# A DFT and MLP sum on Trainium2: the last block's second column pair is turned in two halves, and the last stores change queues

## The chip, the cores and the metric

The kernel runs on one core of a Trainium2 chip. The metric is device time in microseconds. The core has TensorE (matrix products), VectorE (DVE), ScalarE (ACT), GpSimd (POOL) and SyncE (SP). Transfers are started by SP, ACT and GpSimd and are carried by 16 DMA engines.

## The reference

The input is 2048 rows of 640 numbers. After a layer norm the same rows go through two branches, and both are added to the input:

```python
a = einsum("bsd,ed->bse", xn, dft_hid_re);  b = einsum("bsd,ed->bse", xn, dft_hid_im)
y = einsum("ts,bse->bte", dft_seq_re, a) - einsum("ts,bse->bte", dft_seq_im, b)
h = gelu(einsum("bsd,df->bsf", xn, w1) + b1)
return x + y + einsum("bsf,fd->bsd", h, w2) + b2
```

The first branch is the real part of a discrete Fourier transform over rows and columns; the second is an MLP with 1536 hidden units. Everything is float32.

## The kernel before, in words

The 2048 rows are treated as four blocks of 512 rows. Each float32 product is built from three TensorE passes: operands are split in a high and a low part (`split`, lines 160 and 161), and `product` (lines 277 to 279) adds high by high, high by low and low by high. The MLP comes first and leaves its sums, with x added, in DRAM. Then stages over the sequence direction (`sequence_entry`) alternate with stages over the hidden direction (`hidden_entry`), in an order written out by hand: each stage is a list of entries `n`, TensorE's work for the entry is issued first, and then `hidden_beside(b, n)` returns what the other engines do beside it (the dictionary `post`, by entry number). Engines take their instructions in the order in which they were recorded. There is no planner; a semaphore is waited for where one engine needs another's result.

The last stage handles two blocks at once: `ta`, the other block, and `tb`, the last block. Results stand transposed in PSUM banks, 32 x 32 squares at a time, and have to be turned: `turned` (line 1274 for one bank, line 1277 for two) is a VectorE transpose, `add` (line 428) adds the result to the sum that waits in SBUF, and `store` (line 1254) writes it to the output in four DMAs, one for each quarter of the partitions. A block's 160 columns per quarter are five columns of 32: a first pair, a second pair and a fifth column. A store of a pair moves 128 KB per quarter in runs of 256 bytes; a store of one column moves 64 KB in runs of 128 bytes.

In the last entries of the last stage VectorE does, in this order:

- entries 14 and 15: adds to `v2`, turns it and adds it to the first pair of `tb` (`in_two(0)`, tile `u1`); `out_b(0)` stores it from SP;
- entry 17: `v1` (adds a bank pair to the sum `v1`), `end` (adds a turned piece of the other block to a PSUM bank that TensorE still accumulates onto, and waits for), then turns `v1` as one piece of 1024 columns and adds it to the second pair (`in_two(1)`, tile `u2`); `out_b(1)` stores it, four DMAs from ACT;
- entry 18: `yb4` turns and adds the fifth column of `tb` (tile `y4`) and stores it, four DMAs from GpSimd.

Behind the stages (line 1692) the third column of `ta` is turned and added and stored, two DMAs each from SP and ACT. The fourth waits for TensorE's very last product: one transpose (line 1695), then two DMAs each from SP and ACT. At the very end every engine drains (line 1725), SP waits for all DMAs to land, and GpSimd collects the five engines in a barrier. The second load of the tile that is added to, `load_yb(1)`, comes much earlier, in entry 13.

Of the kernel before, what the change touches and what calls it, by code (L numbers as in the profile page):

```python
# [16 lines left out]
Q = 4  # L17
B = 32
# [8 lines left out]
def kernel(  # L27
# [38 lines left out]
    nc = tc.nc  # L66
    x = x.flatten_outer_dims()
    out = out.flatten_outer_dims()
    S, D = x.shape
    F = w1.shape[1]  # L70
    TB = 512
    NT = S // TB
    NB = TB // B
# [4 lines left out]
    DQ = D // Q  # L78
# [27 lines left out]
    def bank(k):  # L106
        return banks[:, k]
# [35 lines left out]
    def place(tag, shape, dtype=F32R, name=None):  # L143

        return wpool.tile(list(shape), dtype, tag=tag, bufs=1, name=name or tag)
# [24 lines left out]
    def rows_of(ap, t):  # L170
        return ap[t * TB : (t + 1) * TB].rearrange("(n r) d -> r n d", r=B)
# [117 lines left out]
    def hidden(g):  # L289
        i = unit(g)  # L290
        acc = bank(g % 3)
        kinds = ((0, 0), (0, 1), (1, 0))
        steps = [(j, k) for j in range(ND) for k in range(3)]
        if g == 0:
            steps = FIRST
        if g == 1:

            steps.sort(key=lambda s: s[1] == 2)
        for n, (j, k) in enumerate(steps):
            a, b = kinds[k]  # L300
            nc.tensor.matmul(  # L301
                acc, W1[i][:, a, j * P : (j + 1) * P], XT[j][:, b], start=n == 0, stop=n == len(steps) - 1
            )
        return acc
# [47 lines left out]
    A = {}  # L352
# [74 lines left out]
    def add(dst, a, b, op=ALU.add):  # L427
        nc.vector.tensor_tensor(dst, a, b, op=op)
# [23 lines left out]
    def load_a(g):  # L452

        for f in steps_of_load(g):
            f()
# [71 lines left out]
    def f5(u):  # L527
        add(held("ci1", u), held("ci1", u), held("ci2", u))

    def f6(u):  # L530
        add(held("cr1", u), held("cr1", u), held("ci1", u))
# [123 lines left out]
    for tag, size, keys in PLACES:  # L655
        t = whole[tag] = place(tag, (P, size // 4))
# [13 lines left out]
    m = MV[:, 1]  # L670
# [132 lines left out]
    for _ in range(5):  # L803
        y, d, x2, z2, w_ = PB[-1]
# [198 lines left out]
    for g in range(NG):  # L1003
        t, i = divmod(g, NF)
        if t == 0:
# [5 lines left out]
            if i == NF - 1:  # L1011
                open_w()
                acc = hidden(g + 2)
# [11 lines left out]
            else:  # L1025
                acc = hidden(g + 2)
# [7 lines left out]
        elif i < NF - 2:  # L1034
            acc = hidden(g + 2)
# [57 lines left out]
    for q in range(1, NF // 2):  # L1093
        p = q - 1
# [100 lines left out]
    for n in range(1, 2 * NF):  # L1195
        blk, i = divmod(n, NF)
# [39 lines left out]
    def load_part(t, k):  # L1236
        nc.sync.dma_start(new_sum(1, t, k), part_of(t, k))
# [10 lines left out]
            for k in names:  # L1248
                nc.sync.dma_start(part_of(t, k), sums[t, k])

    def store(t, src, c0, c1, on_act=0, queues=None):

        for q in range(Q):
            (queues[q] if queues else nc.scalar if q >= Q - on_act else nc.sync).dma_start(
                rows_of(out, t)[:, :, q * DQ + c0 : q * DQ + c1], src[q * B : (q + 1) * B]
            )

    def reload(lo, w, which="xab"):
# [11 lines left out]
    def turned(acc, name):  # L1270

        if len(acc.shape) == 2:
            yt = A["yt"](name)[:, 0]
            nc.vector.transpose(yt, acc)
        else:
            yt = A["yt"](name)
            nc.vector.transpose(yt.rearrange("p e n -> p (e n)"), acc.rearrange("p e n -> p (e n)"))
        return yt

    def add_turned(dst, yt):  # L1280
        if len(yt.shape) == 2:
            add(dst, dst, yt.rearrange("p (n i) -> p n i", i=B))
        else:
            d = dst.rearrange("p n (e i) -> p e n i", i=B)
            add(d, d, yt.rearrange("p e (n i) -> p e n i", i=B))
# [14 lines left out]
    yo = {}  # L1300
# [183 lines left out]
    def hidden_beside(b, n):  # L1484


        ta, tb = blocks[b - 1][1], blocks[b][1]
        last = b == len(blocks) - 1
        x_, y_, z_ = (banks[:, k : k + 2] for k in (X, Y, Z))
        us, vs = bank(US), bank(VS)  # L1490
        ya = yo[ta]

        def s(which, k):
            return sums[(ta, tb)[which], k]

        def t2(k):
            return lambda: add(s(1, KU[k]), s(1, KV[k]), s(1, KU[k]), ALU.subtract)

        def t3(k):
            return lambda: add(s(0, KU[k]), s(1, KU[k]), s(0, KU[k]), ALU.subtract)  # L1500

        def t4(k):
            return lambda: add(s(0, KV[k]), s(0, KV[k]), s(1, KU[k]), ALU.subtract)

        def columns(k):

            return s(1 if last else 0, ("u1", "u2")[k]).rearrange("p a b -> p (a b)").rearrange("p (n e) -> p n e", n=NB)

        def load_yb(k):
            return lambda: nc.sync.dma_start(columns(k), ys[k][tb])  # L1510

        def copy(dst, src):
            return lambda: nc.scalar.activation(dst, src, AF.Copy)

        def to(dst, acc, name, then=lambda: None):


            def f():
                add_turned(dst, turned(acc, name))
                then()  # L1520

            return f

        def out_a(c0, c1):
            return lambda: store(ta, ya[:, :, c0:c1], c0, c1) if last else None

        def odd():
            yt = turned(us, f"yo_{tb}")
            add_turned(ya[:, :, 4 * B :], yt)
            add_turned(yo[tb, 4], yt)  # L1530
            out_a(4 * B, DQ)()

        def in_two(k):

            acc, name = s(1, ("v2", "v1")[k]), f"yb{k}_{tb}"

            def f():
                if name not in A:
                    A[name] = turned(acc, name)
                else:  # L1540
                    add_turned(columns(k), A.pop(name))
                    out_b(k)()

            return f

        def out_b(k):
            return lambda: store(tb, columns(k), 2 * k * B, 2 * (k + 1) * B, Q if last and k == 1 else 0)

        def last_columns():

            A["end"] = A["rt2"][:, 0, 0, 0]
            nc.vector.transpose(A["end"].rearrange("p (n i) -> p n i", i=B), ya[:, :, 3 * B : 4 * B])

        yb1, yb2 = in_two(0), in_two(1)
        yb4 = to(
            yo[tb, 4], vs, f"yb4_{tb}", lambda: store(tb, yo[tb, 4], 4 * B, DQ, queues=[nc.gpsimd] * Q if last else None)
        )
        f5s = [lambda u=u: f5(u) for u in range(2)] if not last else [lambda: None] * 2
        f6s = [lambda u=u: f6(u) for u in range(2)] if not last else [lambda: None] * 2
        v1 = lambda: add(s(1, "v1"), s(1, "v1"), x_)  # L1560
        end = lambda: add(bank(X + 1), bank(X + 1), A["end"])
        pre = [v1] if n == 17 and not last else []
        post = {

            0: [lambda: gather(1, tb, "v1", z_), lambda: gather(1, tb, "v", vs, op=ALU.subtract), f5s[0]],
            1: [f5s[1]],
            3: [to(ya[:, :, : 2 * B], x_, f"ya1_{ta}")],
            2: [last_columns] if last else [],
            4: [t2(0)],
            5: [t2(1)],  # L1570
            6: [to(ya[:, :, : 2 * B], y_, f"ya2_{ta}", out_a(0, 2 * B)), t2(2)],
            7: [odd],
            8: [t3(0)],
            9: [copy(s(1, "v1"), z_), t3(1)],
            10: [t3(2)],
            11: [t4(0)],
            12: [copy(s(1, "v2"), x_), t4(1)],
            13: [load_yb(0), t4(2), load_yb(1)] if last else [t4(2)],
            14: [lambda: add(s(1, "v2"), s(1, "v2"), z_), yb1],
            15: [yb1] if last else [load_yb(0)],  # L1580
            16: [] if last else [load_yb(1)],
            17: [v1, end, yb2, yb2] if last else [yb1, yb2],
            18: [yb4] if last else [yb2],
            19: [f6s[0]],
            20: [] if last else [f6s[1], yb4],
        }.get(n, [])
        if not last:
            if n in (12, 13):
                post.insert(0, lambda: load_g(b, (NW - 1) * ND + 13 - n))
            if n == 18:  # L1590
                post[:0] = [lambda k=k: load_part(blocks[b + 1][1], k) for k in ("u1", "u")]
            if n == 20:
                post.append(lambda: load_a(put_off[0]))

                def end():
                    to(ya[:, :, 2 * B : 4 * B], x_, f"ya3_{ta}")()
                    store(ta, ya, 0, DQ)

                later.append(end)
        return pre, post  # L1600
# [88 lines left out]


    t = blocks[-2][1]
    for k, queues in ((2, [nc.sync, nc.scalar] * 2), (3, [nc.sync, nc.scalar] * 2)):
        d = yo[t][:, :, k * B : (k + 1) * B]
        if k == 3:
            nc.vector.transpose(d, bank(X + 1).rearrange("p (n i) -> p n i", i=B))  # L1695
        else:
            add_turned(d, turned(bank(X), f"yt_{k}"))
        store(t, d, k * B, (k + 1) * B, queues=queues)
# [31 lines left out]
```

## Time and profile before

| | before |
|---|---|
| median of 3 runs | 854.0 us (853.73 to 854.02) |
| profiled execution, device time | 853.7 us |
| profiled execution, span | 851.9 us |
| TensorE busy | 842.7 us, 99% of the span |
| VectorE busy | 661.1 us, 78% |
| ScalarE busy | 353.6 us, 42% |
| GpSimd busy | 48.1 us, 6% |
| GpSimd's last work before the last stores | ends at 298.4 us |
| granted TensorE clock, mean | 0.998 |

The profiled execution is one run; its device time is 1.8 us longer than the span in which its instructions lie. Times in a timeline are microseconds from the span's start. A timeline row has the start, the duration, the engine, the line, the operation, the tile written and the tile read; `x4` means four such instructions merged in one row, and a duration of a DMA row is the time in which it is issued and described, not in which its bytes move. The time from there until the bytes have landed stands in the rows of DMA issues. SPq and ACTq are the queues of SP and ACT; POOL is GpSimd. A drain is an instruction that ends when its engine's earlier work has ended.

### The profile page before, as it was taken

Reading aid. Unit: us, or ns where it says so; the run is one execution under the profiler, and the core shown is the slowest. Engines: PE = TensorE matmul, PEld = TensorE weight load, DVE = VectorE, ACT = ScalarE, POOL = GpSimd, SP = SyncE. Lnnn points to the kernel's source line nnn. Section 1 sums busy time; section 2 is a strip of 40 time slices with the busy share of each in tenths; the row PEclk is TensorE's granted clock in tenths of the full one; section 3 lists DMA queues with packets and bytes.
Section 4 is the critical chain, followed back from the end, with each engine's and each line's share of the span. In section 5 each row is a group of like instructions: output and inputs, shape, how many; then the busy total and the mean of one; then the engine's idle time right before and its main releaser. Section 6 shows DMA issues by size and latency. Waiting matters only on the chain.

```text
span 851.9 us, 10326 instructions
## 1 busy us (share of the span) xinstructions
PE 842.7 (99%) x3711; PEld 695.8 (82%) x3711; DVE 661.1 (78%) x836; ACT 353.6 (42%) x496; POOL 48.1 (6%) x69
## 2 busy tenths in 40 slices
PE   8999999999999999999999999999999999999997
PEld 6888888878888888888888888888888888888885
DVE  7554766785758888879979787889967998885686
ACT  7443634456666554343444343232323423222241
POOL 0000211031211300000000000000000000000001
PEclk9999999999999999999999999999999999999999
DMA  7757698937669998958744679663865779704464
GB/s 186 215 143 199 142 228 233 225 81 190 206 223 349 360 208 161 185 110 200 160 137 105 168 215 293 159 145 97 208 169 169 252 191 228 303 19 179 125 179 99
DMA packets 207235, 158.45 MB, mean 186 GB/s; under 512 B 80848, under 2 KB 180688, under 8 KB 206672
## 3 DMA queue, kind: packets, MB, share of 16 engines
q1 hardware_dynamic: 198880, 136.03, 62.6%
q0 software_dynamic: 4080, 20.97, 6.2%
q10 hardware_dynamic: 4224, 0.79, 0.4%
q8 instruction: 29, 0.48, 0.2%
q14 instruction: 22, 0.18, 0.1%
HBM read 114.76 MB, written 42.99 MB: 185 GB/s over the span
## 4 chain that ended last, share of the span: by engine, by line
PE 98%; DVE 1%; DMA 0%; ACT 0%; issue 0%; SPq 0%; ACTq 0%
PE banks L277 29%; PE banks L279 29%; PE banks L278 29%; PE banks L301 10%; DMA x<-in_A_x_dram 0%; PE banks L667 0%; DVE st L185 0%; ACT ab L672 0%; DVE yo L1695 0%; ACT mv L192 0%; DVE mv L186 0%; DVE xp L208 0%; SPq L178 0%; DVE mv L194 0%; DVE mv L196 0%
## 5 line engine op out<-in xcount | busy, mean ns | idle before, releaser
L277 PE MATMUL banks<-as,xab 128*128 128x512 f32 x411 | 159.9, 389 | 0.0
L279 PE MATMUL banks<-as,xab 128*128 128x512 f32 x411 | 159.9, 389 | 0.0
L278 PE MATMUL banks<-as,xab 128*128 128x512 f32 x411 | 159.9, 389 | 0.0
L160 ACT ACTIVATE as<-r 128x1024 fp32r<-128x1024 f32 x80 | 85.0, 1062 | 177.0 <-PE banks L279 149.2
L161 DVE TENSOR_TENSOR as<-r,as 128x1024 fp32r<-128x1024 f32 x80 | 97.2, 1216 | 41.7 <-ACT as L160 41.6
L278 PEld LDWEIGHTS banks<-as,xab 128*128 128x128 f32 x411 | 77.1, 188 | 16.1
L277 PEld LDWEIGHTS banks<-as,xab 128*128 128x128 f32 x411 | 77.1, 188 | 16.1
L279 PEld LDWEIGHTS banks<-as,xab 128*128 128x128 f32 x411 | 77.1, 188 | 16.0
L277 PE MATMUL banks<-as,xc 128*128 128x512 f32 x224 | 87.1, 389 | 0.0
L278 PE MATMUL banks<-as,xc 128*128 128x512 f32 x224 | 87.1, 389 | 0.0
L279 PE MATMUL banks<-as,xc 128*128 128x512 f32 x224 | 87.1, 389 | 0.0
L160 ACT ACTIVATE as<-rt 128x1024 fp32r<-128x1024 f32 x32 | 34.0, 1063 | 70.8 <-PE banks L279 62.8
L301 PE MATMUL banks<-xtt,xab 128*128 128x512 f32 x240 | 56.9, 390 | 0.0
L301 PEld LDWEIGHTS banks<-xtt,xab 128*128 128x128 f32 x240 | 45.0, 188 | 9.7 <-ACT xtt L160 0.5
L278 PEld LDWEIGHTS banks<-as,xc 128*128 128x128 f32 x224 | 42.0, 188 | 8.8
L279 PEld LDWEIGHTS banks<-as,xc 128*128 128x128 f32 x224 | 42.0, 188 | 8.8
L277 PEld LDWEIGHTS banks<-as,xc 128*128 128x128 f32 x224 | 42.0, 188 | 8.7
L161 DVE TENSOR_TENSOR as<-rt,as 128x1024 fp32r<-128x1024 f32 x32 | 38.8, 1212 | 5.3 <-ACT as L160 5.3
L320 DVE TENSOR_TENSOR hs<-ab,hs 128x512 fp32r<-128x512 f32 x24 | 17.6, 733 | 32.2 <-ACT hs L318 32.2
L160 ACT ACTIVATE as<-u 128x1024 fp32r<-128x1024 f32 (+1 forms) x24 | 22.1, 919 | 48.2 <-PE banks L279 48.2
L488 DVE STREAM_TRANSPOSE r<-raw 128x1024 f32<-128x1024 f32 x32 | 39.5, 1240 | 2.3 <-PE banks L279 1.8
L488 DVE STREAM_TRANSPOSE rt<-raw 128x1024 f32<-128x1024 f32 x32 | 38.8, 1230 | 0.9 <-PE banks L279 0.8
(336 smaller groups left out, 1618.2 us busy)
## 6 DMA issues: line engine op xcount, KB each, us to landing
raw<-in_A_dft_seq_re_dram SPq DMA_DIRECT2D x64, 256.0 KB, 5.8
raw<-in_A_dft_seq_im_dram SPq DMA_DIRECT2D x64, 256.0 KB, 5.1
ws<-wit SPq DMA_DIRECT2D x15, 384.0 KB, 4.1
x<-in_A_x_dram SPq DMA_DIRECT2D x16, 320.0 KB, 4.1
xs<-x SPq DMA_DIRECT2D x64, 80.0 KB, 1.8
xo<-in_A_x_dram SPq DMA_DIRECT2D x16, 320.0 KB, 6.4
xab<-wit SPq DMA_DIRECT2D x13, 384.0 KB, 4.3
wit<-wstp POOLq DMA_DIRECT2D x12, 384.0 KB, 3.9
```

The costliest lines, as they stand in the source:

```text
L160: nc.scalar.activation(h, s, AF.Copy)
L161: nc.vector.tensor_tensor(l, s, h.bitcast(F32), op=ALU.subtract)
L277: nc.tensor.matmul(acc, wh, mh, start=first, stop=False, skip_group_check=goes_on)
L278: nc.tensor.matmul(acc, wh, ml, start=False, stop=False, skip_group_check=goes_on)
L279: nc.tensor.matmul(acc, wl, mh, start=False, stop=last, skip_group_check=goes_on)
L301: nc.tensor.matmul(acc, W1[i][:, a, j * P : (j + 1) * P], XT[j][:, b], start=n == 0, stop=n == len(steps) - 1)
L320: nc.vector.tensor_tensor(hs[:, 1], a, hs[:, 0].bitcast(F32), op=ALU.subtract)
L488: nc.vector.transpose(held(pieces[g][2], u).rearrange("p c (n i) -> p c n i", i=B), r.rearrange("p n (c i) -> p c n i", i=B))
```

## The change

The second pair of the last block is turned and added in two halves. Each half takes half of the rows (8 of the 16 groups of 32) of both columns: two transposes of 128 x 256, one add, one store. `end` stands between the halves. The stores are spread anew:

| store | DMAs before | DMAs after |
|---|---|---|
| first pair of `tb` | 4 SP | 4 GpSimd |
| second pair of `tb` | 4 ACT, whole | first half 2 SP and 2 ACT, second half 4 GpSimd |
| fifth column of `tb` | 4 GpSimd | 2 SP and 2 ACT |
| third column of `ta` | 2 SP and 2 ACT | 1 SP and 3 GpSimd |
| fourth column of `ta` | 2 SP and 2 ACT | the same |

```diff
-    def store(t, src, c0, c1, on_act=0, queues=None):
+    def store(t, src, c0, c1, queues=None, n0=0, n1=NB):
         for q in range(Q):
-            (queues[q] if queues else nc.scalar if q >= Q - on_act else nc.sync).dma_start(
-                rows_of(out, t)[:, :, q * DQ + c0 : q * DQ + c1], src[q * B : (q + 1) * B]
+            (queues[q] if queues else nc.sync).dma_start(
+                rows_of(out, t)[:, n0:n1, q * DQ + c0 : q * DQ + c1], src[q * B : (q + 1) * B, n0:n1]
             )
...
-            return lambda: store(tb, columns(k), 2 * k * B, 2 * (k + 1) * B, Q if last and k == 1 else 0)
+            return lambda: store(tb, columns(k), 2 * k * B, 2 * (k + 1) * B, [nc.gpsimd] * Q if last else None)
+
+        def last_two():
+
+            acc, yt = s(1, "v1"), A["yt"](f"yb2_{tb}")
+            d = columns(1).rearrange("p n (e i) -> p e n i", i=B)
+            v1()
+            for n in range(2):
+                m = slice(n * TB // 2, (n + 1) * TB // 2)
+                for e in range(2):
+                    nc.vector.transpose(yt[:, e, m], acc[:, e, m])
+                dn = d[:, :, n * NB // 2 : (n + 1) * NB // 2]
+                add(dn, dn, yt[:, :, m].rearrange("p e (n i) -> p e n i", i=B))
+                queues = [nc.gpsimd] * Q if n else [nc.sync, nc.scalar] * 2
+                store(tb, columns(1), 2 * B, 4 * B, queues, n * NB // 2, (n + 1) * NB // 2)
+                if n == 0:
+                    end()
...
-            yo[tb, 4], vs, f"yb4_{tb}", lambda: store(tb, yo[tb, 4], 4 * B, DQ, queues=[nc.gpsimd] * Q if last else None)
+            yo[tb, 4], vs, f"yb4_{tb}", lambda: store(tb, yo[tb, 4], 4 * B, DQ, queues=[nc.sync, nc.scalar] * 2 if last else None)
...
-            17: [v1, end, yb2, yb2] if last else [yb1, yb2],
+            17: [last_two] if last else [yb1, yb2],
...
-    for k, queues in ((2, [nc.sync, nc.scalar] * 2), (3, [nc.sync, nc.scalar] * 2)):
+    for k, queues in ((2, [nc.sync, nc.gpsimd, nc.gpsimd, nc.gpsimd]), (3, [nc.sync, nc.scalar] * 2)):
```

## The prediction

> **What bounds the kernel now.** I read the page first: its busy shares and its chain.
>
> ```profile
> span 851.9 us, 10326 instructions
> ...
> PE 842.7 (99%) x3711; PEld 695.8 (82%) x3711; DVE 661.1 (78%) x836; ACT 353.6 (42%) x496; POOL 48.1 (6%) x69
> ...
> PE 98%; DVE 1%; DMA 0%; ACT 0%; issue 0%; SPq 0%; ACTq 0%
> ```
>
> TensorE carries 98% of the chain and the change touches no matmul, so only what happens around the last matmuls can move. The chain in order of time, its last rows:
>
> ```profile
> 845.71 0.24 PE banks L279
> 845.95 0.02 issue
> 845.97 0.72 DVE yo L1695
> ```
>
> TensorE ends at 845.95, one transpose follows, done at 846.69. From there to 851.9 the core computes nothing: 5.2 us of stores, landings and closing. Everything here is decided in the last 14 us, so next comes VectorE's timeline there.
>
> ```profile
> 837.39 1.21 DVE L428 TENSOR_TENSOR v<-v,banks 128x1024 f32<-128x1024 f32 x1
> 838.63 0.70 DVE L428 TENSOR_TENSOR banks<-banks,rt 128x512 f32<-128x512 f32 x1
> 839.24 1.23 DVE L1277 STREAM_TRANSPOSE yb<-v 128x1024 f32<-128x1024 f32 x1
> 840.51 1.23 DVE L428 TENSOR_TENSOR u<-u,yb 128x1024 f32<-128x1024 f32 x1
> 841.84 0.72 DVE L1274 STREAM_TRANSPOSE yb<-banks 128x512 f32<-128x512 f32 x1
> 842.59 0.69 DVE L428 TENSOR_TENSOR y<-y,yb 128x512 f32<-128x512 f32 x1
> 843.39 0.72 DVE L1274 STREAM_TRANSPOSE yt<-banks 128x512 f32<-128x512 f32 x1
> 844.14 0.69 DVE L428 TENSOR_TENSOR yo<-yo,yt 128x512 f32<-128x512 f32 x1
> ```
>
> In order: v1, end, the second pair's turn and add, the last block's fifth column (yb4), the other block's third column. VectorE is full until 844.83 and then waits for TensorE. Next the store queues, in the timelines of SP, ACT and POOL:
>
> ```profile
> 835.76 2.04 SPq L1254 DMA_DIRECT2D out_dram<-u  x4
> 841.77 2.10 ACTq L1254 DMA_DIRECT2D out_dram<-u  x4
> 843.58 2.62 POOL L1254 DMA_DIRECT2D out_dram<-y  x4 [545.20 <-DVE y L428]
> 846.72 0.32 SPq L1254 DMA_DIRECT2D out_dram<-yo  x1
> 846.72 0.37 ACTq L1254 DMA_DIRECT2D out_dram<-yo  x1
> 847.08 1.00 SPq L1254 DMA_DIRECT2D out_dram<-yo  x1
> 847.14 1.04 ACTq L1254 DMA_DIRECT2D out_dram<-yo  x1
> ```
>
> and, in the busy time by stretches, the share of the DMA engines (the last column but one):
>
> ```profile
> 839.00:841.00 2.00, 2.00 (x10) 1.66 (x9) 1.97 (x3) 0.00 (x0) 0.00 (x0) 1.00 0.04 10
> 848.00:849.00 1.00, 0.00 (x0) 0.00 (x0) 0.00 (x0) 0.00 (x0) 0.00 (x0) 1.00 1.08 161
> 849.00:850.00 1.00, 0.00 (x0) 0.00 (x0) 0.00 (x0) 0.00 (x0) 0.00 (x0) 0.56 0.98 145
> 850.00:851.00 1.00, 0.00 (x0) 0.00 (x0) 0.00 (x0) 0.00 (x0) 0.00 (x0) 0.50 0.00 0
> ```
>
> The DMA engines stand still while the second pair is turned, and are full at the end; the two last stores take three times as long to issue as the two before them. Now the landings in us from issue (all four of GpSimd's fifth-column stores, then the last store of each queue alone):
>
> ```profile
> DMA to landing us min/median/max: 2.5/3.0/3.6
> ...
> out_dram<-y POOLq DMA_DIRECT2D x1, 64.0 KB, 3.6
> ...
> out_dram<-yo SPq DMA_DIRECT2D x1, 64.0 KB, 3.3
> out_dram<-yo ACTq DMA_DIRECT2D x1, 64.0 KB, 3.5
> ```
>
> SP's and ACT's last stores land at 847.08 + 3.3 = 850.4 and 847.14 + 3.5 = 850.6. Last, the closing instructions, which the page does not count as busy (ns min/median/max, first and last start):
>
> ```profile
> L1725 SPq DRAIN  x2: 7/7/7, 850.8 to 850.9; - x2
> L1725 POOLq DRAIN  x1: 6171/6171/6171, 845.0 to 845.0; - x1
> ...
> L1725 POOLq EVENT_SEMAPHORE  x1: 17/17/17, 851.2 to 851.2; - x1
> ```
>
> This view decides the forecast. GpSimd collects the other engines before the program closes. SP, which has waited for all landings, arrives at 850.9. GpSimd's own drain runs 6.17 us and ends at 851.2, and its collecting instruction follows at once. So SP's landings do not end the kernel: GpSimd's drain does, by 0.3 us. Its last store was described at 843.58 + 2.62 = 846.2 and landed at 845.6 + 3.6 = 849.2; the drain ends 5.0 us after the first and 2.0 us after the second. At the program's start the same instruction, with no store behind it, took:
>
> ```profile
> L1716 POOLq DRAIN  x1: 182/182/182, 0.3 to 0.3; - x1
> ```
>
> **The change, part by part.** It is summed against the profiled execution: 853.7, 1.8 more than its span and 0.3 below the median, 854.0.
>
> *First pair to GpSimd.* Four stores leave SP at 835.76 for GpSimd. SP waits for nothing else there, and the DMA engines idle afterwards: cover enough. GpSimd's price for a store:
>
> ```profile
> L1254 POOL DMA_DIRECT2D out_dram<-y x4: 648/654/693, 843.6 to 845.6; - x4
> L1144 POOL DMA_DIRECT2D forms_c<-xcst x4 | 2.1, 531 | 8.0 <-DVE xcst L428 8.0
> ```
>
> I take 0.65, which these have in common with the new ones: 32 partitions and short runs; 0.53 is the low end. Four end near 836.0 + 2.6 = 838.6, before GpSimd's next work. Nothing.
>
> *Second pair in halves.* VectorE loses one transpose and one add of 1024 columns (1.23 each) and gets four transposes of 256 columns and two adds of 512. No row has a 256-column transpose: 512 cost 0.72 and 1024 cost 1.23, so the straight line gives 0.465; the ends are 1.23 / 4 = 0.31 and 0.72 (no gain from the smaller size). The line is nearest. Four are 1.86, two adds 2 x 0.69 = 1.38: 3.24 for 2.46, so VectorE runs 0.8 later from here (0.2 to 1.8). Where that lies: end moves from before the pair to between the halves, to about 838.6 + 0.93 + 0.69 = 840.2 to 840.9. TensorE needs it for the last column's 15 matmuls, 15 x 0.23 = 3.45 before 845.95, at 842.5: 1.6 to spare. The third column's add ends at 844.83 + 0.8 = 845.6; the last transpose waits for TensorE until 845.97, so 0.35 us of cover is left and the 0.8 costs nothing there. If the small transposes cost 0.72, the add ends at 846.6 and the last transpose goes 0.65 late.
>
> *The halves' stores.* The first half's four (half the bytes) issue on SP and ACT at 840.2 instead of 841.8, into idle DMA engines, and free 256 KB of the final rush. The second half goes to GpSimd: its add ends at 841.74 + 0.8 = 842.5, GpSimd starts 0.3 later (it did so after the fifth column's add: 842.59 + 0.69 = 843.28, then 843.58), and 4 x 0.65 end at 845.4, before it is needed again. Hidden.
>
> *Fifth column to SP and ACT.* Two issues each, at 844.1, of 0.3 to 0.5 us (as the stores of this size at 846.72); both are free again before 846.7. In the built order SP's very last store also waits until ACT's first fifth-column store has landed, because they share a counter: at 2.5 to 3.0 to landing (GpSimd's for the same bytes, above) that is 846.6 to 847.1 against its issue at 847.08. Nothing; at 3.6 it would be 0.6 late, the high end.
>
> *Third column.* Three of its four stores go from SP and ACT to GpSimd. They wait for the add at 845.6, start at 845.9, and end at 845.9 + 3 x 0.65 = 847.85. The last starts at 847.2 and, at 3.0 to 3.6 to landing, lands at 850.2 to 850.8. So GpSimd's last description ends 1.6 later than in the profile (847.85 for 846.2), its last landing 1.0 to 1.6 later (for 849.2).
>
> *The end.* SP's and ACT's last two stores now find fewer bytes before them. Their second issue may shrink from 1.0 to the 0.35 of the first, and they land at best like an unhurried store,
>
> ```profile
> out_dram<-u SPq DMA_DIRECT2D x4, 128.0 KB, 2.3
> ```
>
> at 847.1 + 2.3 = 849.4 rather than 850.6: a gain of 0 to 1.2 on the path through SP, 0.4 by my guess since GpSimd's third column is still in flight. It is worth nothing if GpSimd's drain ends later. By either yardstick, 5.0 after the last description or 2.0 after the last landing, the drain moves by 1.0 to 1.6 and ends at 852.2 to 852.8. Sum: 0 + 0 + 0 + 1.0 to 1.6; I take 1.2, nearer the landing yardstick because the rush at the end is lighter. The time is 854.0 + 1.2 = 855.2.
>
> The Trainium skill, "Perfetto Trace Analysis", § Per-engine timelines, says that the profiler shows only the execution of a drain and not its wait for semaphores. By that the 6.17 us would be GpSimd's own work; the trace agrees in so far as the collecting instruction follows within a tenth of a microsecond. The Trainium skill, "DMA: Bandwidth & Descriptors", § Issuing engines are not separate DMA queues, says that DMAs of all issuers share the same 16 engines and that issuing from several saves only issue time. By that the choice of queue would be worth nothing but the issue time, and the sum would be near 854.0. The 0.98 to 1.08 share in the last two busy microseconds agrees with the shared engines; the drain row is what the rule leaves out.
>
> **The rivals.**
> 1. *The drain does not follow GpSimd's stores* (it may wait until all transfers are quiet: 850.6 + 0.6). Then the lighter rush counts: -0.2 to -1.2, 853.6 by the middle guess of 0.4, 852.8 at the extreme. For it: the drain ended only 0.3 after SP, and the DMA row shows real crowding. Against: 182 ns at the start without stores, and no quiet-time reason is visible. This is the one on the faster side; it decides as soon as the drain ends before SP's last landing plus 0.3.
> 2. *The drain counts stores.* Four stores from 843.58 to 851.2 are 1.9 us each if it is a backlog worked off one by one; eleven from 836.0 would end at 856.9, 5.7 later: 859.7. For it: the numbers fit one row. Against: landings of 2.5 to 3.6 us after four issues 0.65 apart show no such queue in the transfers.
> 3. *The halves are dear.* Small transposes at 0.72: GpSimd's last store is described at 846.6 + 0.3 + 1.95 = 848.85, the drain ends 2.65 later: 856.7.
> 4. *The change does not do what it says*: the add of the second half could have to wait until the first half's stores have read their tile. In the built order it waits for VectorE alone, so I give this nothing.
>
> **How the numbers follow.** The forecast (drain +1.0 to +1.6) has 0.58, rival 1 0.27, rival 2 0.08, rival 3 0.07. The range runs from 853.3, which leaves out the lower part of rival 1 (0.08), to 856.2, which leaves out rivals 2 and most of 3 (0.13). The forecast's own range is 854.8 to 855.8. A change under 0.2% (1.7 us) is about what this measurement cannot tell from none. Slower by more: rivals 2 and 3 and a tenth of the range's top, 0.24. Faster by more would need 852.3, beyond even rival 1's extreme: 0.03. Within: 0.73.
>
> **What will show it.** GpSimd's drain row should begin near 847 and end at 852.2 to 852.8, with SP's drain before it. VectorE's third-column add should end near 845.6 and the last transpose still start at 845.97 behind TensorE. The pair of 256-column transposes should read near 0.47 each. GpSimd's last three stores should start near 845.9. SP's and ACT's last issue should fall below 1.0. I am wrong if the drain ends within 1 us of SP's last landing whatever GpSimd stored, or if the last transpose starts after 846.1.

## The result and the profile after

The changed kernel takes 854.99 us (median of 22 runs, 854.74 to 856.78) against 854.00 us (22 runs, 853.62 to 855.06): a ratio of 1.0012 [1.0007, 1.0018], 1.0 us more. The square brackets hold a 95% interval; it leaves out 1, so a change of 0.12% can be told from none here. The forecast was 855.2. The profiled execution of the changed kernel took 855.2 us.

The page of the changed kernel, its header, busy shares and chain:

```profile
span 853.4 us, 10337 instructions
PE 843.1 (99%) x3711; PEld 696.0 (82%) x3711; DVE 661.6 (78%) x840; ACT 353.1 (41%) x496; POOL 52.5 (6%) x76
...
PE 92%; DVE 3%; DMA 1%; issue 1%; POOL 1%; ACT 1%; SPq 0%; POOLq 0%; DVEq 0%; ACTq 0%
```

TensorE's busy time is what it was (842.7 before). The chain that ended last now has POOL and POOLq in it, which it did not have before. Its last rows, in order of time, show why:

```profile
840.00 0.69 DVE u L428
840.70 0.61 DVE banks L428
841.30 0.68 DVE yb L1557 x2
...
845.11 0.70 DVE yo L428
845.81 0.28 issue
846.09 1.29 POOL out_dram L1254 x2
847.38 0.64 POOLq L1741
```

Before, the chain's last rows were TensorE's last product and the last transpose. Now TensorE's last product is not on it. It runs through VectorE (the two halves with `end` between them, then the fifth column and the third column's add) to GpSimd's third-column stores, and from there into GpSimd's closing. The closing instructions of the changed kernel (line 1741; ns min/median/max, first and last start), and GpSimd's stores with their landings:

```profile
L1741 POOLq DRAIN  x1: 5669/5669/5669, 847.0 to 847.0; - x1
...
L1741 SPq DRAIN  x2: 7/7/7, 851.6 to 851.7; - x2
...
L1741 POOLq EVENT_SEMAPHORE  x4: 17/17/17, 852.7 to 853.3; - x4
```

```profile
L1254 POOL DMA_DIRECT2D out_dram<-u x8: 584/618/696, 836.6 to 844.7; - x8
...
L1254 POOL DMA_DIRECT2D out_dram<-yo x3: 651/651/651, 846.1 to 847.4; - x3
...
DMA to landing us min/median/max: 2.0/2.5/3.0
```

SP is through at 851.7. GpSimd's drain ends at 847.0 + 5.67 = 852.7, and its collecting instruction follows at once: SP waits 0.96 us for GpSimd, where it was 0.24 before. GpSimd's last store starts at 847.4 and lands 3.0 later, at 850.4; the drain ends 2.3 after that.

One correction is needed before times of two traces are set side by side. In this execution TensorE ended at 846.47, 0.54 later than in the one before (845.93). The matmuls are the same, and over the profiles of all the timed kernels below TensorE ends anywhere from 845.87 to 846.81, the latest of them in a kernel with a shorter median than before's. So this is a difference between executions, and I measure the tail from TensorE's end:

| us after TensorE's end | before | after | difference |
|---|---|---|---|
| GpSimd's last store described | 0.27 | 1.56 | +1.29 |
| GpSimd's last landing | 3.24 | 3.93 | +0.69 |
| GpSimd's drain ends | 5.21 | 6.19 | +0.98 |
| SP is through | 4.97 | 5.23 | +0.26 |
| the span ends | 5.99 | 6.96 | +0.97 |

The span's 0.97 is the median's 1.0, and the drain's 0.98 accounts for it.

### The profile page after: what moved, and what is told of

It reads as the page before. It is cut to its first block, busy times and chain, and to the rows that moved or that the text cites. A ratio compares the mean times of both kernels' runs of the same rounds, so it can differ in the third digit from the quotient of the medians.

```text
span 853.4 us, 10337 instructions
## 1 busy us (share of the span) xinstructions
PE 843.1 (99%) x3711; PEld 696.0 (82%) x3711; DVE 661.6 (78%) x840; ACT 353.1 (41%) x496; POOL 52.5 (6%) x76
## 4 chain that ended last, share of the span: by engine, by line
PE 92%; DVE 3%; DMA 1%; issue 1%; POOL 1%; ACT 1%; SPq 0%; POOLq 0%; DVEq 0%; ACTq 0%
PE banks L277 27%; PE banks L278 27%; PE banks L279 27%; PE banks L301 10%; DMA wz<-in_A_dft_hid_im_dram 1%; POOL xo L349 1%; DVE as L161 1%; DMA ys<-xo 0%; DMA x<-in_A_x_dram 0%; SPq L364 0%; DVE v L428 0%; DVE u L428 0%; PE banks L667 0%; DVE st L185 0%; DVE rq L428 0%
```

## The experiments

The theory was the prediction's: the program ends when the later of two is through, SP (which waits for all landings) or GpSimd's drain, and GpSimd's drain follows GpSimd's own stores, by their description or by their landing. The rivals: the drain follows something else (all transfers being quiet, or a backlog of stores worked off one by one); or the time comes from the halves and from the path through SP, whatever GpSimd does. Each edit has its name in brackets, with the kernel that it starts from. Behind each time stands its ratio to the runs of before on the same chip, with the 95% interval. The runs of before on the same chips had medians of 853.76 (first four kernels), 853.95 (next three) and 853.76 (last two).

**The third column back on SP and ACT** (third_back, against after):

```diff
-    for k, queues in ((2, [nc.sync, nc.gpsimd, nc.gpsimd, nc.gpsimd]), (3, [nc.sync, nc.scalar] * 2)):
+    for k, queues in ((2, [nc.sync, nc.scalar] * 2), (3, [nc.sync, nc.scalar] * 2)):
```

> The changed kernel with the third column's four stores back on SP and ACT, two each; everything else as changed, so GpSimd's last store is the second half of the pair. If GpSimd's closing drain follows its own last store (4.6 to 5.0 us after the last description, 2.0 to 2.3 us after the last landing, by the two profiles), it ends near 845.3 + 5 = 850.3 or earlier, no longer last, and the time falls by 1.0 us or more from the changed kernel: 853.6 to 854.0. If the drain ends only when all transfers are quiet, it stays behind SP's drain as in both profiles and the time falls by less than 0.4 us: 854.6 or more. If the drain counts stores (eight here, eleven in the changed kernel), it ends 3 stores earlier but still after SP's.

853.50 us, 0.9997 [0.9988, 1.0006]. Its closing instructions:

```profile
L1741 POOLq DRAIN  x1: 5407/5407/5407, 844.7 to 844.7; - x1
...
L1741 SPq DRAIN  x3: 7/7/7, 851.7 to 852.1; - x3
...
L1741 POOLq EVENT_SEMAPHORE  x4: 17/17/17, 851.8 to 852.5; - x4
```

The drain is over at 850.1 and GpSimd then waits until SP is through at 851.8. So the drain is not tied to all transfers being quiet; it followed GpSimd's stores back by almost three microseconds. The loss of the change is gone, and no more than the loss: SP's path, 4.99 after TensorE's end, is no shorter than before's 4.97.

**The third column alone** (third_only, against before):

```diff
-    for k, queues in ((2, [nc.sync, nc.scalar] * 2), (3, [nc.sync, nc.scalar] * 2)):
+    for k, queues in ((2, [nc.sync, nc.gpsimd, nc.gpsimd, nc.gpsimd]), (3, [nc.sync, nc.scalar] * 2)):
```

> The kernel before with one edit: three of the third column's four stores on GpSimd, behind the fifth column's four. GpSimd's last description then ends at 846.2 + 3 x 0.65 = 848.2, 2.0 us later than before. If the drain follows the last description the time is 856.0; if it follows the last landing (launched at 847.5, landing 2.5 to 3.6 later, 850.0 to 851.1 for 849.2), 854.8 to 855.9. If the drain does not follow GpSimd's stores, 853.6 to 854.2. If it counts stores, seven for four, at 1.9 us each: 859.7.

855.48 us, 1.0021 [1.0012, 1.0030], the slowest timed kernel here. Its closing:

```profile
L1725 SPq DRAIN  x2: 7/7/7, 851.7 to 851.8; - x2
L1725 POOLq DRAIN  x1: 6319/6319/6319, 846.6 to 846.6; - x1
...
L1725 POOLq EVENT_SEMAPHORE  x1: 17/17/17, 852.9 to 852.9; - x1
```

GpSimd ends at 846.6 + 6.32 = 852.9, 1.1 behind SP, and the span ends 7.65 after TensorE's end, 1.66 later than before's (the median: +1.72). Here the fifth column's four stores stand ahead of the third column's three on GpSimd, which therefore start at 846.3. This part of the change alone makes the loss, without any halves.

**No store of the tail on GpSimd** (no_gpsimd, against after):

```diff
-            return lambda: store(tb, columns(k), 2 * k * B, 2 * (k + 1) * B, [nc.gpsimd] * Q if last else None)
+            return lambda: store(tb, columns(k), 2 * k * B, 2 * (k + 1) * B, None)
...
-                queues = [nc.gpsimd] * Q if n else [nc.sync, nc.scalar] * 2
+                queues = [nc.sync, nc.scalar] * 2
...
-    for k, queues in ((2, [nc.sync, nc.gpsimd, nc.gpsimd, nc.gpsimd]), (3, [nc.sync, nc.scalar] * 2)):
+    for k, queues in ((2, [nc.sync, nc.scalar] * 2), (3, [nc.sync, nc.scalar] * 2)):
```

> The halves as in the changed kernel, but no store of the last stage on GpSimd: first pair on SP, both halves, fifth column and third column on SP and ACT, two each. If the drain follows GpSimd's last store, it takes a fraction of a microsecond (0.18 us at the program's start) and SP's landings set the end: 0.3 us below the kernel before by the drain alone, less what more bytes on SP and ACT cost, 853.3 to 854.2. If the drain waits for all transfers, it still ends last, about 0.5 us or more after SP's last landing, and the time is that of the kernel before or above.

854.51 us, 1.0009 [1.0000, 1.0018], above the 853.3 to 854.2 that were expected if the drain follows GpSimd's stores. GpSimd's long drain did move to the middle of the kernel, behind its last transfer there, but the tail still got longer: the expectation had left out what follows. SP's timeline; the same for 841.5 to 843.5 alone, where its two stores of the first half stand; SP's waits (us in total, times, longest); and ACT's stores of the two halves:

```profile
835.98 10.01 SPq L1254 DMA_DIRECT2D out_dram<-u  x8
...
847.80 2.14 SPq L1254 DMA_DIRECT2D out_dram<-yo  x4
```

```profile
842.19 0.81 SPq L1254 DMA_DIRECT2D out_dram<-u  x2
```

```profile
SPq L1254 <- DMA out_dram<-u: 5.8, 2, 4.1
```

```profile
840.38 2.83 ACTq L1254 DMA_DIRECT2D out_dram<-u  x4
```

SP issues the first pair's four stores from 835.98 to 838.0, and its four for the halves only by 845.99; the waits say that it stood 5.8 us for stores of `u` to land (both pairs' tiles have that name in a profile). In the built order, SP's and ACT's stores take turns on eight completion counters (a counter tells that a store has landed), and a store waits until the store that had its counter before has landed. The stores that SP stood for are not those of the first pair, as the expectation of first_only below has it: these landed 2.0 to 2.3 us after their issue, so before 840. They are ACT's. SP's first store of the first half has the counter of ACT's first one, issued at 840.38 and landed 1.8 later, and SP goes on at 842.2, 1.8 us after the data was ready; its first store of the second half waits in the same way until 844.7 for one that ACT issued at 842.7. SP stays late after that: its first issue for the last two columns is at 847.80.

**The halves alone** (halves_only, against before: the pair in halves as in the change, with before's queues):

```diff
-                queues = [nc.gpsimd] * Q if n else [nc.sync, nc.scalar] * 2
+                queues = [nc.scalar] * Q
```

(the first pair on SP, the fifth column on GpSimd, the third on SP and ACT).

> The kernel before with the second pair turned, added and stored in two halves, all eight stores on ACT; the fifth column on GpSimd and the third on SP and ACT as before. VectorE runs 0.5 us later from the pair on (two 256-column transposes take 0.77 together in the changed kernel's profile), so GpSimd's fifth column starts and ends 0.5 us later: if the drain follows GpSimd's last store the time is 854.0 + 0.5, 854.3 to 854.7. If SP's last landing or all transfers set the end, the earlier first half gives 0 to 0.4 us back: 853.6 to 854.0.

854.34 us, 1.0007 [0.9998, 1.0016]; the span ends 6.55 after TensorE's end, 0.56 later than before's. The time lies in the range that was expected if the drain sets the end, but not by that path: the drain moved by 0.3 (5.50 for 5.21), and SP is through later, at 5.80 (4.97 before). The last transpose still waits for TensorE, so this is no price of VectorE's. ACT has eight stores for the halves, and its first store of the fourth column is issued late (the last row is SP's first store of the third column):

```profile
840.10 3.93 ACTq L1254 DMA_DIRECT2D out_dram<-u  x8
...
847.52 1.16 ACTq L1254 DMA_DIRECT2D out_dram<-yo  x2
```

```profile
845.20 0.32 SPq L1254 DMA_DIRECT2D out_dram<-yo  x1
```

That is at 847.52; SP's was at 846.65, after the same transpose. ACT's queue was not full: its store before that had been described by 846.2. In the built order the four more stores shift the counters, so that ACT's store now has the counter of SP's first third-column store, which was issued at 845.20 and landed 2.2 later, at 847.4. So the cost of the halves shows here in a wait for a shared counter, and not on VectorE.

**The fifth column split** (fifth_split, against third_back): GpSimd keeps two stores of the fifth column behind the second half's four.

```diff
-    lambda: store(tb, yo[tb, 4], 4 * B, DQ, queues=[nc.sync, nc.scalar] * 2 if last else None)
+    lambda: store(tb, yo[tb, 4], 4 * B, DQ, queues=[nc.sync, nc.scalar, nc.gpsimd, nc.gpsimd] if last else None)
```

> The kernel third_back (changed kernel, third column back on SP and ACT) with two of the fifth column's four stores on GpSimd behind the second half, one each left on SP and ACT. GpSimd's last description then ends about 1.3 us later than in third_back, its drain about 4.5 us after that, some 4.7 us behind TensorE's end and just before SP's drain (5.0 there). If the end is set by whichever of the two drains is later, and by bytes and shared counters on SP and ACT, the time is 0.1 to 0.4 us below third_back: 853.1 to 853.5. If the drain counts or crowds more than that, it becomes last again: 853.8 or more.

853.70 us, 0.9998 [0.9989, 1.0007]. It was expected 0.1 to 0.4 below third_back and is not: both are 0.3 below before's runs on their own chips. GpSimd's last store is described at 846.13, lands at 848.43, and the drain ends at 850.65: 4.52 after the first, 2.22 after the second. SP is through at 851.23 and ends the kernel. The 5.0 of the prediction would have put the drain at 851.1; this speaks for the landing, weakly.

**The first pair alone on GpSimd** (first_only, against third_back): the halves all go to SP and ACT.

```diff
-                queues = [nc.gpsimd] * Q if n else [nc.sync, nc.scalar] * 2
+                queues = [nc.sync, nc.scalar] * 2
```

> The changed kernel with only the first pair on GpSimd; both halves, the fifth and the third column on SP and ACT, two each. GpSimd's drain should end near 844, far from the end. Beside no_gpsimd this takes four stores off SP. If shared counters held SP up there (SP waits 5.8 us for landings of the first pair's stores in its profile), the time falls below no_gpsimd's: 853.4 to 854.0. If only the number of bytes on SP and ACT counts, it stays near no_gpsimd: 854.3 or more.

852.87 us, 0.9986 [0.9977, 0.9995]: faster than before by 1.1 us and than the changed kernel by 2.1, and below the range that was expected. Its closing and SP's timeline:

```profile
L1741 POOLq DRAIN  x3: 40/102/5378, 837.5 to 850.8; - x3
L1741 SPq DRAIN  x3: 7/7/7, 850.3 to 850.6; - x3
```

```profile
840.20 2.82 SPq L1254 DMA_DIRECT2D out_dram<-u  x4
843.75 0.85 SPq L1254 DMA_DIRECT2D out_dram<-y  x2
845.29 2.33 SPq L1254 DMA_DIRECT2D out_dram<-yo  x4
```

GpSimd's drain starts at 837.5 and is over at 842.8, more than seven microseconds before it could matter. SP issues each store as soon as its data is there, and is through 4.36 after TensorE's end (4.97 before). From the kernel without GpSimd in the tail this one differs only in the queue of the first pair's four stores. That is 1.1 us after TensorE's end (5.13 against 6.25) and 1.6 us of median, on two chips whose medians of before differ by 0.2. From third_back it differs only in the queue of the second half's four stores. On GpSimd they are described from 843.3 to 845.6 and the last lands 1.16 after TensorE's end; on SP and ACT they are described from 842.2 to 843.1 and have landed by 844.8, 1.2 before TensorE's end. That is 0.63 us of span after TensorE's end (5.76 against 5.13), with GpSimd's drain last in neither.

**Four big copies on GpSimd in the middle** (big_early, against no_gpsimd). They copy the input to a spare tensor; the result does not need them.

```diff
+            for k in range(4):
+                nc.gpsimd.dma_start(spare[k * TB : (k + 1) * TB], x[k * TB : (k + 1) * TB])
```

> The kernel no_gpsimd with four copies of 1.3 MB each, from the input to a spare array, on GpSimd behind its last additions near 298 us; they are the last work of GpSimd, and the drain follows them in the middle of the kernel, with nothing waiting for it. The copies add work that the result does not need. Four copies of 1.3 MB take far longer to land than to describe (4 x 0.6 us). If the drain waits for the landing of GpSimd's transfers, it ends 2.0 to 2.3 us after the last landing, 15 us or more after the last description. If it is a fixed piece of work after GpSimd's last instruction, it ends 3.8 to 5.0 us after the last description, with the copies still in flight.

864.05 us, one run; the time is not the point, and why it is 9.5 us above no_gpsimd's was not looked into. It is here for the drain. The four copies, their landings, and the drain behind them:

```profile
L1166 POOL DMA_DIRECT2D spare<-in_A_x_dram x4: 491/498/537, 298.4 to 299.9; - x4
...
DMA to landing us min/median/max: 8.3/14.0/19.6
...
L1744 POOLq DRAIN  x1: 23475/23475/23475, 298.1 to 298.1; - x1
```

The last copy is described at 300.4 and lands at 299.9 + 19.6 = 319.5. The drain ends at 298.1 + 23.5 = 321.5: 21 us after the last description, 2.0 after the last landing. That settles the yardstick. Without the copies, the same drain followed one forms store:

```profile
L1741 POOLq DRAIN  x1: 5686/5686/5686, 296.7 to 296.7; - x1
```

It ended at 302.4, 1.8 after that store had landed (300.6).

**First pair and third column on GpSimd** (first_third, against after: the second half goes to SP and ACT).

```diff
-                queues = [nc.gpsimd] * Q if n else [nc.sync, nc.scalar] * 2
+                queues = [nc.sync, nc.scalar] * 2
```

> The kernel first_only with three of the third column's stores on GpSimd, as in the changed kernel: one step alone, the one the prediction priced. In first_only SP's drain is 4.4 us behind TensorE's end and GpSimd's drain far away. If GpSimd's drain ends 2.0 to 2.3 us after its last landing, it ends 5.9 to 6.3 us behind TensorE's end as in the changed kernel, and the time is that of the changed kernel although the second half is no longer on GpSimd: 854.6 to 855.1, 1.7 to 2.2 above first_only. If lighter traffic of SP and ACT counted, it would stay below 853.5.

854.69 us, 1.0014 [1.0005, 1.0022]. Its closing:

```profile
L1741 SPq DRAIN  x2: 7/7/7, 850.8 to 850.8; - x2
...
L1741 POOLq DRAIN  x1: 5422/5422/5422, 846.4 to 846.4; - x1
```

SP is through at 850.8, GpSimd at 851.8. Seven stores on GpSimd, or eleven as in the changed kernel, make little difference (the drain ends 5.91 and 6.19 after TensorE's end; 854.69 and 854.99 us): what counts is the last landing, at 3.82 and 3.93. From first_only, the fastest kernel here, it differs only in the three third-column stores, which cost 1.8 us of median (two chips) and 1.6 after TensorE's end (6.69 against 5.13).

**The best kernel with the pair whole** (first_whole, against first_only):

```diff
-            17: [last_two] if last else [yb1, yb2],
+            17: [v1, end, yb2, yb2] if last else [yb1, yb2],
```

(its second pair is stored by SP and ACT, two each).

> The kernel first_only with the second pair whole again: turned, added and stored in one piece, two stores each on SP and ACT, which are four stores fewer. It tells what the halves are worth where GpSimd's drain is out of the way. If starting half of the pair 1.6 us earlier shortens the rush at the end, the time is 0.3 to 1.0 us above first_only: 853.2 to 853.9. If the rush is decided by the fifth, third and fourth column alone, it is the same or, with 0.5 us less on VectorE, lower: 852.4 to 852.9.

853.71 us, 0.9998 [0.9989, 1.0007]: the halves are worth 0.7 us once the drain is out of the way (the span after TensorE's end, 5.83 against 5.13), or 0.84 us by the medians, from two chips. The busy time by stretches, the last column but one the DMA share: first of the kernel with halves, then of the one with the pair whole.

```profile
840.00:842.00 2.00, 2.00 (x11) 1.65 (x10) 1.97 (x5) 0.00 (x0) 0.00 (x0) 1.00 0.49 122
...
848.00:850.00 2.00, 0.00 (x0) 0.00 (x0) 0.00 (x0) 0.00 (x0) 0.00 (x0) 1.00 0.63 99
```

```profile
840.00:842.00 2.00, 2.00 (x11) 1.65 (x10) 1.97 (x2) 0.00 (x0) 0.00 (x0) 1.00 0.18 41
...
848.00:850.00 2.00, 0.00 (x0) 0.00 (x0) 0.00 (x0) 0.00 (x0) 0.00 (x0) 0.96 1.27 145
```

With halves, the DMA engines work at 840 to 842, when they are otherwise nearly idle, and the last rush is lighter by half. With the pair whole, the later landings also hold up stores by their counters. These are SP's waits in that kernel; with halves it has none of them:

```profile
SPq L1254 <- DMA out_dram<-u: 1.1, 2, 0.7
SPq L1254 <- DMA out_dram<-y: 0.8, 2, 0.6
```

ACT's last store is held up too: it starts 1.84 after TensorE's end with the pair whole and 1.20 with halves.

All the timed kernels together, in us after TensorE's end of each one's profiled execution:

| kernel | GpSimd's last landing | its drain ends | SP is through | span ends | which ends it | median, us |
|---|---|---|---|---|---|---|
| before | 3.24 | 5.21 | 4.97 | 5.99 | drain | 854.00 |
| after | 3.93 | 6.19 | 5.23 | 6.96 | drain | 854.99 |
| third column alone | 4.79 | 6.88 | 5.78 | 7.65 | drain | 855.48 |
| first pair and third column | 3.82 | 5.91 | 4.90 | 6.69 | drain | 854.69 |
| halves alone | 3.53 | 5.50 | 5.80 | 6.55 | SP | 854.34 |
| third column back | 1.16 | 3.30 | 4.99 | 5.76 | SP | 853.50 |
| fifth column split | 2.40 | 4.62 | 5.20 | 5.96 | SP | 853.70 |
| first pair, pair whole | -5.15 | -3.18 | 5.07 | 5.83 | SP | 853.71 |
| first pair alone | -5.11 | -3.13 | 4.36 | 5.13 | SP | 852.87 |
| none on GpSimd | | | 5.48 | 6.25 | SP | 854.51 |

In every row the span ends 0.75 to 0.78 after the later of drain and SP, and the drain ends 1.97 to 2.26 after the last landing. These last differences go with the number of stores that GpSimd issued behind its last computation: 1.97 or 1.98 with four (also behind the four big copies), 2.09 with seven (two kernels), 2.14 with eight, 2.22 with ten, 2.26 with eleven, and 1.81 with none (the drain at 302.4 above): 0.04 us for each store.

## Why the prediction was right, point by point

- **The end** carried the forecast, and its mechanism held: GpSimd's drain closes the kernel and moved by 0.98 with GpSimd's stores. Of its two yardsticks, which gave the same answer before, the landing is the right one (21 us after the description with the big copies). The size, 1.2 forecast and 0.98 measured, just misses the low end of the forecast's 1.0 to 1.6. That it comes so close is in part luck: the last landing moved by 0.69 only, less than the 1.0 to 1.6 that were forecast for it, and the other 0.29 is a term that the forecast did not have, the 0.04 us for each of seven more stores on GpSimd.
- **The third column** is why that size is a little high. The stores were forecast to start at 845.9 and end at 847.85. They ended at 848.02, but 1.56 after TensorE's end where the forecast amounts to 1.9: VectorE delayed them less than assumed. The last landed 3.0 after its issue, the low end of the 3.0 to 3.6 that were assumed. Three at 0.65 and the 0.3 between add and first store were as forecast.
- **The halves**: forecast 0.8 on VectorE; measured 0.4 at the third column's add (845.80 for 844.83, less 0.54 for the execution). VectorE's timeline after the change:

```profile
839.20 0.77 DVE L1557 STREAM_TRANSPOSE yb<-v 128x256 f32<-128x256 f32 x2
840.00 0.69 DVE L428 TENSOR_TENSOR u<-u,yb 128x512 f32<-128x512 f32 x1
...
841.21 0.76 DVE L1557 STREAM_TRANSPOSE yb<-v 128x256 f32<-128x256 f32 x2
842.01 0.69 DVE L428 TENSOR_TENSOR u<-u,yb 128x512 f32<-128x512 f32 x1
...
845.11 0.69 DVE L428 TENSOR_TENSOR yo<-yo,yt 128x512 f32<-128x512 f32 x1
846.50 0.72 DVE L1711 STREAM_TRANSPOSE yo<-banks 128x512 f32<-128x512 f32 x1 [0.71 <-PE banks L279]
```

  Two 256-column transposes in a row take 0.77, not 0.93: the straight line through the two larger sizes overstated the small one. The last transpose starts at 846.50, past the 846.1 that I had named as a sign of being wrong. But it waits 0.71 for TensorE, which ended later in this execution; the sign should have been that wait, not a clock time.
- **The second half on GpSimd** was hidden, as forecast; each store took 0.58 instead of 0.65.
- **The first pair** was priced at nothing. As a cost that is right. As a gain it is the step that I missed, though only beside other stores' queues: in first_only against no_gpsimd it is worth 1.1 to 1.6 us, because SP's later stores no longer wait on counters that ACT's stores hold. The changed kernel does not have this gain. It has no such waits in SP's queue either, but SP is through only at 5.23 after TensorE's end; with the second half back on SP and ACT as well as the third column it is 4.36.
- **The path through SP** was to gain 0.4. SP's and ACT's last issues shrank as forecast:

```profile
847.61 0.51 SPq L1254 DMA_DIRECT2D out_dram<-yo  x1
...
847.66 0.58 ACTq L1254 DMA_DIRECT2D out_dram<-yo  x1
```

  Yet SP was through 5.23 after TensorE's end, 0.26 later than before, so this guess fell. The forecast did not rest on it. The step that failed is that a shorter issue and fewer bytes ahead would let the last stores land sooner. ACT's very last store, the last to land in both kernels, still takes 3.5 us from issue (847.66 + 3.5 = 851.2; 847.14 + 3.5 = 850.6 before), which is 4.7 after TensorE's end in both:

```profile
out_dram<-yo ACTq DMA_DIRECT2D x1, 64.0 KB, 3.5
```

  The 0.26 lies behind the landings. SP waits for the counters one after another, and in the built order that store's counter now comes earlier in the row: SP is through 0.5 us after the last landing, where it was 0.3 before. The DMA share by stretches in the changed kernel shows why the rush is no lighter:

```profile
843.00:844.00 1.00, 1.00 (x6) 0.84 (x5) 0.97 (x2) 0.00 (x0) 1.00 (x2) 1.00 0.00 0
...
849.00:850.00 1.00, 0.00 (x0) 0.00 (x0) 0.00 (x0) 0.00 (x0) 0.00 (x0) 0.74 1.09 198
850.00:851.00 1.00, 0.00 (x0) 0.00 (x0) 0.00 (x0) 0.00 (x0) 0.00 (x0) 0.50 0.31 47
```

  At 843 to 844 nothing moves, while GpSimd is still describing the second half. The rush was moved, not lightened: first_only against third_back prices the second half's late start on GpSimd at 0.63 us.
- **The rivals.** The drain that does not follow GpSimd's stores is excluded by third_back against after. The drain that counts stores at 1.9 us each is excluded by seven against eleven stores, and by four copies that took 21 us; what is left of it is the 0.04 us for each store. That moving stores between queues changes nothing but issue time, near 854.0, is excluded by the third column alone: 1.72 us above before. The dear halves are excluded by the 0.77. That the adds wait for the stores did not show in VectorE's timeline.

## What to carry to other kernels

This kernel ended when the later of two closing paths ended: look for each engine's drain at the end of the trace, not only for the last landing. A store from GpSimd delayed the end when it landed less than about 2 us before SP was through; the first pair's stores, seven microseconds earlier, cost nothing on GpSimd. Look also at which stores share a completion counter: a store can stand with its data ready until a store of another engine has landed. Splitting a late store paid where it filled idle DMA time (0.7 us in first_only), and did not where the extra stores made a queue wait on a shared counter (0.6 us lost in halves_only).

## What the hardware showed that I had not expected

- GpSimd's closing drain lasted until about 2 us (1.8 to 2.3 in eleven traces) after the last landing of GpSimd's own transfers, 1.81 us and 0.04 us for each store behind its last computation. Why it grows with the stores is open. One behind four 1280 KB copies lasted 23.5 us.
- SP's queue stood 5.8 us in two waits in no_gpsimd, some 3.5 us of it with the data ready, for stores of ACT to land. This comes from the built order of the counters and not from the queue itself: in first_only it has no such wait.
- GpSimd's price for a store went by the number of runs rather than bytes here: 0.65 us for 512 runs, of 256 bytes (first pair) and of 128 bytes (third column) alike, 0.58 for 256 runs of 256 bytes (a half), and 0.50 for a copy of 1280 KB.
